# Input weights as two words: adding them on TensorE instead of GpSimd, in a three-layer attention and gating kernel

## The chip, the cores and the metric

The kernel runs on one core of one Trainium2 chip. The metric is the device time of one launch in microseconds, the median of the timed executions; it is to be small. The engines are named as in the profile: PE is TensorE's matmul, PEld its weight load, DVE is VectorE, ACT is ScalarE, POOL is GpSimd, SP is SyncE, which issues the DMAs here.

## The reference, cut to what matters

Three layers follow one another: an attention with two kinds of masks, a gated layer with a mixing over positions, and a mixture of four attention experts.

```python
q, k, v            # 4 batches, 8 heads, 576 positions, 64 columns, float32
a = softmax(where(mask_h, q @ k.T / 8, -1e9))     # heads 0-3: last 32 positions
x = concat_heads(a @ v)                           # heads 4-7: every 32nd position
h = maximum(x @ w_in, 0)                          # w_in: 512 x 1024, float64
u, v = h[..., :512], h[..., 512:]
v_n = (v - mean(v)) / sqrt(var(v) + 1e-6)
v_s = einsum('ts,bsd->btd', w_spatial, v_n) + b_spatial[None, :, None]
y = (u * v_s) @ w_out                             # w_out: 512 x 512, float64
# four experts: q, k, v = y @ wq[e], y @ wk[e], y @ wv[e]; causal attention;
# out = sum over the two experts with the largest gate of w_e * (a @ v @ wo[e])
```

In the first softmax the sum of a row gets 1e-9 added before it is inverted. The weights `w_in` and `w_out` come as float64, so a weight is read as two 32-bit words.

## The kernel before, in words

Every dense product is made of three matmuls on float32r operands: each operand is held as an upper part (`hi`, `wh`) and a remainder (`lo`, `wl`), and `mm3` (lines 274 to 283) adds hi by hi, lo by hi and hi by lo in one PSUM bank.

The order of all instructions is fixed when the program is built. A planner (class `Plan`, lines 33 to 148) takes steps from generators; a step yields the engine, or several to choose from with a cost each, the events it needs and the buffers it takes, and the planner gives each engine a list in the order in which the steps would start by these costs. So an engine runs its own list strictly in order and waits on semaphores for the others. The classes of buffers are `c` (75 tiles in SBUF), `w64` (raw weight words), `d`, `s`, `t`, `x` (the eight PSUM banks).

The first stage has two jobs side by side. For each of four head pairs of a batch the first attention runs: SP loads q, k and v, PE makes scores (line 467), DVE masks them and finds maxima (line 493), ACT takes the exponentials with row sums (line 499), DVE adds 1e-9 to the sums and inverts them (lines 502 and 503), POOL or DVE multiplies (line 506), PE transposes (line 524) and multiplies by v (line 565), and ACT and DVE split the result into `xh` and `xl` (lines 302 and 588). Meanwhile the eight tiles of `w_in`, 128 rows by 512 columns each, are prepared by `weight`. A tile of raw words is loaded into one of two `w64` buffers (line 329). DVE builds the value of its upper word as a float32 `a` in two instructions (336, 337), a power of two `p2` (338), and the remainder `m` from the lower word (341). Then the two are added on DVE or POOL (344), the sum is rounded to `hi` (302 on ACT, 304 on DVE or POOL), and `m` less `hi` gives `wl` on DVE or POOL (351). PE fills its idle time until a planned 46 us with matmuls on zeros (line 213).

The first dense products are `v_half` of batch 0 (lines 281 to 283, 512 columns), which need the second half of `w_in`, then `u_half` (288 columns), which needs all of the first half, and then the mixing over positions (`spatial`, lines 730 to 735). The attention of batch 1 is prepared by then, and from there on the batches follow each other. `w_out` and the experts' weights are prepared later, with the same function; `w_out` is float64 too.

Of the kernel before, what the change touches and what calls it, by code (L numbers as in the profile page):

```python
# [7 lines left out]
F = dt.float32  # L8
R = dt.float32r
I32 = dt.int32  # L10
AF = mybir.ActivationFunctionType
ALU = mybir.AluOpType
# [6 lines left out]
NCHUNK = 75  # L19
EXPERTS_AHEAD = 4  # L20
TAILS = 3
ALONE = 3
# [127 lines left out]
def fused(tc, qk, vl, vs, win, wsb, woutT, wp, wo, out):  # L150
# [5 lines left out]
        tc.tile_pool(name="ps", bufs=1, space=bass.MemoryType.PSUM),  # L156
    ]
    const, chunk, small, psum = [c.__enter__() for c in ctx]
    plan = Plan(dict(c=NCHUNK, w64=2, bd=TAILS, al=ALONE, ps=8, sq=PSUM_BANKS["d"] - 1, **PSUM_BANKS))
    plan.within = dict.fromkeys(PSUM_BANKS, "ps")  # L160

    n_names = [0]
# [1 line left out]
    def nm(s):  # L164
        n_names[0] += 1
        return f"{s}{n_names[0]}"

    def C(shape, dtype=F, name="c"):
        return chunk.tile(shape, dtype, name=nm(name), tag="c")

    def P(shape, tag):
        t = psum.tile([128, 512], F, name=nm("p" + tag), tag="p", bufs=8)
        n = 1
        for x in shape[1:]:
            n *= x
        t = t[: shape[0], :n]
        if len(shape) == 3:
            t = t.rearrange("p (a b) -> p a b", b=shape[2])
        return t
# [4 lines left out]
    def f(t):  # L184
        return t.bitcast(F)
# [7 lines left out]
    def t_dve(n, k=1, fixed=0.07):  # L193
        return k * fixed + n * 1.042e-3
# [4 lines left out]
    def t_pool(n, k=1):  # L199
        return k * 0.15 + n * 2.1e-3  # L200

    def t_mm(n, k):
        return k * max(n * 0.4167e-3 + 0.003, 0.056)
# [13 lines left out]

    ident = const.tile([128, 128], F, name="ident")
    make_identity(nc, ident)

    def keep(t, pattern, base, mult, cmp_op=ALU.is_ge, fill=NEG):
        pool.affine_select(t, t, pattern=pattern, base=base, channel_multiplier=mult, compare_op=cmp_op, fill=fill)
# [70 lines left out]
    def hi_of(n):  # L293
        return ("act", "dve", "pool"), (t_act(n), t_fast(n), t_pool(n))


    def out_of(n, k=1):
        return ("act", "dve"), (t_act(n, k), t_dve(n, k))

    def copy(out, in_):  # L300
        if plan.eng == "act":
            act.activation(out, in_, AF.Copy)  # L302
        else:
            engine().tensor_copy(out, in_)  # L304
# [7 lines left out]
    W = {}  # L312


    def weight(keys, src, r0, rows, c0, cols, after=()):


        n = len(keys)
        if src.dtype == F:
            yield "sp", 0.46, after, dict(c=1)  # L320
            m = C([rows, n * cols], F, "st")
            nc.sync.dma_start(m.rearrange("p (a c) -> p a c", a=n),
                              src[r0:r0 + n * rows, c0:c0 + cols].rearrange("(a p) c -> p a c", a=n))
            plan.dma(n * rows * cols * 4)
            plan.lat = 0.0
        else:
            yield "sp", 0.46, after, dict(w64=1)
            w = chunk.tile([rows, cols, 2], I32, name=nm("w64"), tag="w64", bufs=2)
            nc.sync.dma_start(w.rearrange("p a b -> p (a b)"),
                              src.bitcast(I32)[r0:r0 + rows, 2 * c0:2 * (c0 + cols)])  # L330
            plan.dma(rows * cols * 8)


            yield "dve", t_fast(2 * cols, 2) + t_dve(cols) + 0.25, (), dict(c=2)
            a, p2 = C([rows, cols], I32, "a"), C([rows, cols], I32, "p2")
            dve.tensor_scalar(a, w[:, :, 1], 3, 0x3FFFFFFF, op0=ALU.logical_shift_left, op1=ALU.bitwise_and)
            dve.scalar_tensor_tensor(a, w[:, :, 1], -0x40000000, a, op0=ALU.bitwise_and, op1=ALU.bitwise_or)
            dve.tensor_scalar(p2, a, -0x800000, None, op0=ALU.bitwise_and)
            yield "dve", t_dve(cols), (), dict(c=1)
            m = C([rows, cols], F, "m")  # L340
            engine().scalar_tensor_tensor(m, w[:, :, 0].bitcast(dt.uint32), 2.0 ** -52, f(p2), op0=ALU.mult, op1=ALU.mult)
            plan.give("w64")
            yield ("dve", "pool"), (t_dve(cols), t_pool(cols)), (), {}
            engine().tensor_add(m, m, f(a))
            plan.give("c", 2)
        yield *hi_of(n * cols), (), dict(c=1)
        hi = C([rows, n * cols], R, "wh")
        copy(hi, m)
        yield *lo_of(n * cols), (), dict(c=1)
        wl = C([rows, n * cols], R, "wl")  # L350
        engine().tensor_sub(wl, m, f(hi))
        plan.give("c")
        for i, key in enumerate(keys):
            W[key] = (hi[:, i * cols:i * cols + cols], wl[:, i * cols:i * cols + cols])
            plan.set(("W", key))
# [115 lines left out]
    def a1_weights(b, hp, g):  # L471
        local = hp < 2
        blocks = a1_blocks(hp, g)
        n = len(blocks)
        nk = 96 if local else 54
        width = [96 if local else min(54, S - 54 * j) for j in blocks]
        if not local:
            yield "pool", 0.25 + 0.25 * g, [("qk", b, hp)], dict(c=1)
            a = C([128, n + n % 2, 64], F, "a")
            pool.memset(a[:, :, 54:], 0.0)  # L480
            if g:
                pool.memset(a[:, 5, 36:], 0.0)
                pool.memset(a[:, 7, :54], 0.0)
        yield "dve", t_dve(n * nk, n), [("mask", local), ("s1", b, hp)], dict(c=1) if local else {}
        st = A1[b, hp]
        ps = st["ps"][g]

        mx = sm([128, 8], "mx")
        if local:
            a = C([128, n, nk], F, "a")  # L490
        for c, (j, w) in enumerate(zip(blocks, width)):
            m = mloc[:, min(j, 1)] if local else mstl if w == 36 else mstr
            dve.tensor_tensor_reduce(a[:, c, :w], ps[:, c, :w], m, op0=ALU.add, op1=ALU.min, scale=-0.125,  # L493
                                     scalar=3.0e38, accum_out=mx[:, c:c + 1])
        plan.give("s")
        yield "act", t_act(n * nk, n, 0.23), (), {}
        sums = sm([128, 8], "sums")
        for j, w in enumerate(width):
            act.activation(a[:, j, :w], a[:, j, :w], AF.Exp, bias=mx[:, j:j + 1], scale=-1.0,  # L499
                           accum_out=sums[:, j:j + 1])  # L500
        yield "dve", 0.3, (), {}
        dve.tensor_scalar_add(sums[:, :n], sums[:, :n], 1e-9)
        dve.reciprocal(sums[:, :n], sums[:, :n])
        yield ("dve", "pool"), (t_dve(n * nk), t_pool(n * nk)), (), {}
        x = a[:, :n, :nk]
        engine().tensor_mul(x, x, sums[:, :n].unsqueeze(2).broadcast_to([128, n, nk]))  # L506
        st["a"][g] = a
        plan.set(("a", b, hp, g))
# [656 lines left out]
    attention(0, 0)  # L1165
    for h in (1, 0):
        for k in range(4):
            plan.add(-0.5 + k if h else 2 + k, weight([("in", h, k)], win, 128 * k, 128, 512 * h, 512, after=() if h else ()))
    for s in range(4):
        plan.add(30, weight([("sp", s)], wsb, 128 * s, 128, 0, S, after=[("x",0,2,0)]))  # L1170
    plan.add(30, spatial_tail())
# [117 lines left out]
```

## Time and profile before

| | us |
|---|---|
| median of 3 timed runs | 456.47 (456.34 to 456.61) |
| the profiled execution's own time | 455.08 |
| span of the profiled execution | 453.2 |
| PE busy | 426.1 (94%) |
| DVE busy | 320.2 (71%) |
| ACT busy | 289.2 (64%) |
| POOL busy | 160.5 (35%) |

The span runs from the first instruction of the program to the last; the execution's own time holds what lies around it as well. The busy times are unions of instruction times on each engine. A busy PE is not a PE at its peak, since matmuls overlap and their ends are modelled, and the matmuls on zeros count as busy too.

### The profile page before, as it was taken

The page shows a single profiled execution, that of the slowest core. Times are in us where ns is not written, and L with a number is a line of the kernel's source. Part 1 is how long each engine was busy: PE and PEld are TensorE (multiplying, and loading weights), DVE is VectorE, ACT ScalarE, POOL GpSimd, SP SyncE. Part 2 cuts the span into 40 slices and gives each one's busy share as a digit, 9 for nine tenths or more (in the row PEclk, how much of TensorE's full clock was granted, in tenths as well). Part 3 has the DMA queues.
Part 4 walks back from the last instruction along what each step waited for, and adds up shares of the span by engine and source line. Part 5 has one row for each costly group of instructions (what it writes and reads, how often), then busy time and mean ns, then how long its engine had stood idle before and what let it go on. Part 6 is the DMA issues. An engine that isn't in the chain of part 4 may idle for free.

```text
span 453.2 us, 10964 instructions
## 1 busy us (share of the span) xinstructions
PE 426.1 (94%) x3872; PEld 382.7 (84%) x3872; DVE 320.2 (71%) x1145; ACT 289.2 (64%) x922; POOL 160.5 (35%) x248
## 2 busy tenths in 40 slices
PE   5786599999999999999999999999999999999796
PEld 2464478998899889999999999989998999988684
DVE  5999988246922485233999755679879898988861
ACT  3786789228950498331644433986878788878873
POOL 7766986022720163013669910102001222103200
PEclk9998989999999999999999999999999999999999
DMA  8988307300165000220200033810550370051234
GB/s 265 360 258 258 79 26 235 101 2 2 42 209 203 2 1 4 60 105 25 59 35 1 0 83 71 191 42 16 128 116 3 80 175 3 0 144 56 94 116 140
DMA packets 22554, 42.96 MB, mean 95 GB/s; under 512 B 3170, under 2 KB 5474, under 8 KB 22500
## 3 DMA queue, kind: packets, MB, share of 16 engines
q1 hardware_dynamic: 22500, 42.26, 32.8%
q8 instruction: 31, 0.51, 0.5%
q14 instruction: 23, 0.19, 0.1%
HBM read 26.00 MB, written 4.72 MB: 68 GB/s over the span
## 4 chain that ended last, share of the span: by engine, by line
PE 79%; DVE 11%; ACT 3%; POOL 3%; issue 2%; DMA 1%; POOLq 0%; ACTq 0%; DVEq 0%
PE pd L281 15%; PE pd L283 15%; PE pd L282 15%; PE pd L730 4%; PE pd L732 4%; PE pd L731 4%; PE pt L1010 4%; PE px L1055 2%; PE ps L925 2%; PE ps L926 2%; PE px L565 2%; PE pt L524 2%; PE px L1085 2%; PE px L1053 2%; PE ps L467 2%
## 5 line engine op out<-in xcount | busy, mean ns | idle before, releaser
L499 ACT ACTIVATE a<-a,mx 128x54 f32<-128x54 f32 (+2 forms) x160 | 54.4, 345 | 23.1 <-DVE mx L493 22.8
L946 POOL TENSOR_SCALAR a<-a,asums 128x128 f32<-128x128 f32 (+2 forms) x18 | 14.3, 802 | 96.5 <-ACT a L937 27.5
L738 DVE TENSOR_TENSOR u<-pd,u 128x288 f32<-128x288 f32 x32 | 14.2, 453 | 36.4 <-PE pd L735 36.2
L937 ACT ACTIVATE a<-a,amx 128x128 f32<-128x128 f32 (+1 forms) x64 | 35.5, 556 | 6.5 <-DVE amx L913 6.2
L281 PE MATMUL pd<-xh,wh 128*128 128x288 f32 x128 | 38.7, 302 | 0.1
L281 PE MATMUL pd<-gh,fh 128*128 128x288 f32 x128 | 38.0, 297 | 0.7 <-DVE cl L1070 0.7
L913 DVE CUSTOM_DVE_ANT_0 a<-ps,mqk 128x128 f32<-128x128 f32 (+4 forms) x72 | 33.0, 482 | 7.2 <-PE ps L926 5.7
L506 POOL TENSOR_TENSOR a<-a,sums 128x384 f32<-128x384 f32 (+3 forms) x30 | 24.7, 824 | 37.3 <-ACT a L499 14.1
L283 PE MATMUL pd<-gh,fl 128*128 128x288 f32 x128 | 37.9, 296 | 0.0
L730 PE MATMUL pd<-wh,vh 128*128 128x288 f32 x128 | 37.8, 295 | 0.0
L283 PE MATMUL pd<-xh,wl 128*128 128x288 f32 x128 | 37.7, 295 | 0.0
L282 PE MATMUL pd<-xl,wh 128*128 128x288 f32 x128 | 37.7, 294 | 0.0
L732 PE MATMUL pd<-wh,vlo 128*128 128x288 f32 x128 | 37.7, 294 | 0.0
L282 PE MATMUL pd<-gl,fh 128*128 128x288 f32 x128 | 37.7, 294 | 0.0
L731 PE MATMUL pd<-wl,vh 128*128 128x288 f32 x128 | 37.7, 294 | 0.0
L499 ACT ACTIVATION_READ_ACCUMULATOR a<-a,mx 128x1 f32 x160 | 30.5, 190 | 0.0
L999 DVE TENSOR_TENSOR e<-pt,e 128x384 fp32r<-128x384 f32 (+1 forms) x48 | 27.4, 597 | 4.0 <-ACT e L302 3.6
L281 PE MATMUL pd<-wh,xh 128*128 128x512 f32 x64 | 27.7, 432 | 0.4 <-DVE aT L304 0.4
L944 ACT ACTIVATE a<-a,asums 128x512 f32<-128x512 f32 (+3 forms) x46 | 26.5, 595 | 2.3 <-DVE asums L954 2.0
L653 POOL TENSOR_TENSOR rstd<-rstd,neghalf 128x1 f32<-128x1 f32 x18 | 11.5, 636 | 40.7 <-DVE rstd L651 25.7
L282 PE MATMUL pd<-wl,xh 128*128 128x512 f32 x64 | 25.7, 401 | 0.0
L283 PE MATMUL pd<-wh,xl 128*128 128x512 f32 x64 | 25.6, 399 | 0.0
(208 smaller groups left out, 1464.1 us busy)
## 6 DMA issues: line engine op xcount, KB each, us to landing
qk<-qk SPq DMA_DIRECT2D x64, 144.0 KB, 2.6
q<-in_qk_dram SPq DMA_DIRECT2D x16, 288.0 KB, 5.4
k<-in_qk_dram SPq DMA_DIRECT2D x16, 288.0 KB, 5.7
w<-in_win_dram SPq DMA_DIRECT2D x8, 512.0 KB, 5.7
out_dram<-o SPq DMA_DIRECT2D x16, 256.0 KB, 2.0
v<-in_vl_dram SPq DMA_DIRECT2D x16, 192.0 KB, 4.7
v<-in_vs_dram SPq DMA_DIRECT2D x8, 256.0 KB, 5.8
w<-in_woutT_dram SPq DMA_DIRECT2D x4, 512.0 KB, 6.4
```

The source lines that it names most:

```text
L281: pe.matmul(ps, ah, bh, start=i == 0, stop=False)
L282: pe.matmul(ps, ah, bl, start=False, stop=False)
L283: pe.matmul(ps, al, bh, start=False, stop=i == n - 1)
L499: act.activation(a[:, j, :w], a[:, j, :w], AF.Exp, bias=mx[:, j:j + 1], scale=-1.0, accum_out=sums[:, j:j + 1])
L506: engine().tensor_mul(x, x, sums[:, :n].unsqueeze(2).broadcast_to([128, n, nk]))
L730: pe.matmul(ps, vh[:, fs], wh[:, c0:c0 + cn], start=(i == 0), stop=False)
L731: pe.matmul(ps, vh[:, fs], wl[:, c0:c0 + cn], start=False, stop=False)
L732: pe.matmul(ps, vlo[:, fs], wh[:, c0:c0 + cn], start=False, stop=False)
L913: dve.tensor_tensor_reduce(a[:, s0:s0 + sn], ps, mask, op0=ALU.add, op1=ALU.min, scale=-0.125, scalar=m if s0 else 3.0e38, accum_out=m)
L937: act.activation(a, a, AF.Exp, bias=m, scale=-1.0, accum_out=st["sums", e][:, i:i + 1])
L944: act.activation(a, a, AF.Copy, scale=r)
L999: dve.tensor_sub(el, ps, f(eh))
```

## The change

For the eight tiles of `w_in` alone (`summed=True`) the sum is no longer made on POOL or DVE. `hi` is the rounded `a`, not the rounded sum. PE adds `a` times the identity, `m` times an identity in float32r and `hi` times a negative identity in one PSUM bank, and what stands there is copied out by ACT or DVE as `wl`. The first of these three matmuls takes float32 operands. `m` is now written as float32r. Two constants, `unit` and `minus`, are made by DVE at the start. The raw words have three buffers instead of two, for `w_in` and `w_out`. And the addition of 1e-9 to the row sums is written as an instruction that has the sums as both of its tensor inputs, (sums + 1e-9) max sums.

```diff
-    plan = Plan(dict(c=NCHUNK, w64=2, bd=TAILS, al=ALONE, ps=8, sq=PSUM_BANKS["d"] - 1, **PSUM_BANKS))
+    plan = Plan(dict(c=NCHUNK, w64=3, bd=TAILS, al=ALONE, ps=8, sq=PSUM_BANKS["d"] - 1, **PSUM_BANKS))
...
     make_identity(nc, ident)
+    unit, minus = (const.tile([128, 128], R, name=n) for n in ("unit", "minus"))
+    dve.tensor_copy(unit, ident)
+    dve.tensor_scalar_mul(minus, ident, -1.0)
...
-            w = chunk.tile([rows, cols, 2], I32, name=nm("w64"), tag="w64", bufs=2)
+            w = chunk.tile([rows, cols, 2], I32, name=nm("w64"), tag="w64", bufs=3)
...
-            m = C([rows, cols], F, "m")
+            m = C([rows, cols], R if summed else F, "m")
             engine().scalar_tensor_tensor(m, w[:, :, 0].bitcast(dt.uint32), 2.0 ** -52, f(p2), op0=ALU.mult, op1=ALU.mult)
             plan.give("w64")
+            if summed:
+                yield *hi_of(cols), (), dict(c=1)
+                hi = C([rows, cols], R, "wh")
+                copy(hi, f(a))
+                yield "pe", t_mm(cols, 6), (), dict(d=1)
+                ps = P([rows, cols], "d")
+                pe.matmul(ps, ident, f(a), start=True, stop=False)
+                pe.matmul(ps, unit, m, start=False, stop=False)
+                pe.matmul(ps, minus, hi, start=False, stop=True)
+                plan.give("c", 3)
+                yield *out_of(cols), (), dict(c=1)
+                wl = C([rows, cols], R, "wl")
+                copy(wl, ps)
+                plan.give("d")
+                key, = keys
+                W[key] = (hi, wl)
+                plan.set(("W", key))
+                return
             yield ("dve", "pool"), (t_dve(cols), t_pool(cols)), (), {}
             engine().tensor_add(m, m, f(a))
...
-        dve.tensor_scalar_add(sums[:, :n], sums[:, :n], 1e-9)
+        dve.scalar_tensor_tensor(sums[:, :n], sums[:, :n], 1e-9, sums[:, :n], op0=ALU.add, op1=ALU.max)
...
-            plan.add(-0.5 + k if h else 2 + k, weight([("in", h, k)], win, 128 * k, 128, 512 * h, 512, after=() if h else ()))
+            plan.add(-0.5 + k if h else 2 + k, weight([("in", h, k)], win, 128 * k, 128, 512 * h, 512, summed=True))
```

The planner makes the engines' lists anew. On POOL, at the end of the constants of the first stage (`mstl` is the last mask), before:

```order
L222 AFFINE_SELECT mstl<-mstl 64x36
L344 TENSOR_TENSOR m_174<-m_174,a_160 128x512
L351 TENSOR_TENSOR wl_246<-m_174,wh_230 128x512
L506 TENSOR_TENSOR a_213<-a_213,sums_233 128x480
L344 TENSOR_TENSOR m_284<-m_284,a_239 128x512
L506 TENSOR_TENSOR a_225<-a_225,sums_250 128x384
L351 TENSOR_TENSOR wl_352<-m_284,wh_314 128x512
```

and now (line numbers are the changed kernel's; 527 is the multiplication by the inverted sums, 501 to 504 are memsets):

```order
L225 AFFINE_SELECT mstl<-mstl 64x36
L527 TENSOR_TENSOR a_218<-a_218,sums_238 128x480
L527 TENSOR_TENSOR a_233<-a_233,sums_261 128x384
L501 MEMSET a_355 128x4x10
L501 MEMSET a_359 128x8x10
L503 MEMSET a_359 128x28
L504 MEMSET a_359 128x54
```

The additions of line 344 and the subtractions of line 351 are gone for all eight tiles of `w_in`; the multiplications that stood between them follow each other. Three of the eight roundings to `wh` come to POOL instead, later in its list.

On DVE, at the second tile of raw words, after the first nine maxima; before:

```order
L336 TENSOR_SCALAR a_239<-w_154 128x512
L337 SCALAR_TENSOR_TENSOR a_239<-w_154,a_239 128x512
L338 TENSOR_SCALAR p_240<-a_239 128x512
L502 TENSOR_SCALAR sums_233<-sums_233 128x5
L503 RECIPROCAL sums_233<-sums_233 128x5
L341 SCALAR_TENSOR_TENSOR m_284<-w_154,p_240 128x512
L502 TENSOR_SCALAR sums_250<-sums_250 128x4
L503 RECIPROCAL sums_250<-sums_250 128x4
```

and now:

```order
L339 TENSOR_SCALAR a_247<-w_158 128x512
L340 SCALAR_TENSOR_TENSOR a_247<-w_158,a_247 128x512
L341 TENSOR_SCALAR p_248<-a_247 128x512
L523 SCALAR_TENSOR_TENSOR sums_238<-sums_238 128x5
L524 RECIPROCAL sums_238<-sums_238 128x5
L344 SCALAR_TENSOR_TENSOR m_266<-w_158,p_248 128x512
L339 TENSOR_SCALAR a_269<-w_160 128x512
L340 SCALAR_TENSOR_TENSOR a_269<-w_160,a_269 128x512
L341 TENSOR_SCALAR p_270<-a_269 128x512
L523 SCALAR_TENSOR_TENSOR sums_261<-sums_261 128x4
L524 RECIPROCAL sums_261<-sums_261 128x4
L344 SCALAR_TENSOR_TENSOR m_307<-w_160,p_270 128x512
```

The third tile's four instructions (`w_160`, `a_269`, `p_270`, `m_307`) have moved up by nine maxima, to right behind the second's, and `sums` is added in the other form. The order of the engines' later work changes in the same manner; over the list up to the first maxima of batch 1's third head pair the work on DVE is the same but for one copy `wl<-pd`, one copy `xh<-px` of 256 columns and one multiplication of 384 columns more, and one copy `aT<-pt` of 256 columns less.

On PE, between the scores of the second and of the third head pair; before:

```order
L213 MATMUL pd_69<-zeros 128x512
L524 MATMUL pt_300<-ident,a_213 96x128 x4
L213 LDWEIGHTS zeros
L213 MATMUL pd_69<-zeros 128x512
L213 LDWEIGHTS zeros
L213 MATMUL pd_69<-zeros 128x512
L524 MATMUL pt_318<-ident,a_213 96x128
L467 MATMUL ps_320<-k_172,q_171 64x54
```

and now:

```order
L488 MATMUL ps_285<-k_163,q_162 64x96 x2
L545 MATMUL pt_309<-ident,a_218 96x128 x4
L352 MATMUL pd_315<-a_247,ident 128x512
L353 MATMUL pd_315<-m_266,unit 128x512
L354 MATMUL pd_315<-wh_276,minus 128x512
L545 MATMUL pt_348<-ident,a_218 96x128
L545 MATMUL pt_350<-ident,a_233 96x128 x4
L352 MATMUL pd_363<-a_269,ident 128x512
L353 MATMUL pd_363<-m_307,unit 128x512
L354 MATMUL pd_363<-wh_330,minus 128x512
L488 MATMUL ps_379<-k_210,q_209 64x54
```

The three matmuls of the second and of the third tile stand ahead of the third pair's scores, where matmuls on zeros were. Up to the first matmul of `spatial` PE's list has eight such groups of three more and 15 matmuls on zeros less (21 instead of 36), and is otherwise made of the same instructions.

## Rows read from the trace of the kernel before

**Rows 1.** Busy time by stretch: busy us (instructions), then PEclk, DMA share, GB/s.
```profile
2.00:45.00 43.00, 31.42 (x477) 20.37 (x476) 37.74 (x156) 27.75 (x130) 29.60 (x50) 0.97 0.94 297
4.70:57.30 52.60, 36.47 (x567) 25.14 (x567) 49.90 (x211) 36.26 (x158) 38.55 (x51) 0.95 0.80 248
85.80:292.00 206.20, 206.20 (x1928) 192.97 (x1927) 122.56 (x418) 104.94 (x348) 75.82 (x103) 1.00 0.21 59
```

**Rows 2.** Chain that ended last, 20 to 62 us, shares by line.
```profile
by line: DVE a L493 17.2%; DVE p L338 12.0%; DVE xl L588 10.0%; DVE a L337 9.5%; DVE a L336 9.2%; DVE sums L502 7.4%; issue 7.1%; DVE wl L351 5.9%; DVE m L341 5.9%; DVE a L506 4.3%; DVE xt L304 3.5%; DVE sums L503 3.4%; DVE bst L647 1.7%; D
```

**Rows 3.** Groups by shape, 4.7 to 57.3 us: busy us, mean ns, idle before.
```profile
L351 POOL TENSOR_TENSOR wl<-m,wh 128x512 fp32r<-128x512 f32 x8 | 11.5, 1438 | 2.0 <-ACT wh L302 1.8
...
L344 POOL TENSOR_TENSOR m<-m,a 128x512 f32<-128x512 f32 x8 | 10.6, 1329 | 5.5 <-DVE sums L502 3.5 <-DVE m L341 1.9
L213 PE MATMUL pd<-zeros 128*128 128x512 bf16 x27 | 8.1, 389 | 0.0
L336 DVE TENSOR_SCALAR a<-w 128x512 int32<-128x512 int32 x8 | 7.5, 935 | 3.9 <-DMA w<-in_win_dram 3.9
...
L341 DVE SCALAR_TENSOR_TENSOR m<-w,p 128x512 f32<-128x512 uint32 x8 | 6.4, 805 | 0.0
L338 DVE TENSOR_SCALAR p<-a 128x512 int32<-128x512 int32 x8 | 6.3, 788 | 0.3
...
L302 ACT ACTIVATE wh<-m 128x512 fp32r<-128x512 f32 x8 | 5.0, 626 | 9.3 <-POOL m L344 9.3
...
L502 DVE TENSOR_SCALAR sums<-sums 128x4 f32<-128x4 f32 x6 | 2.8, 469 | 0.0
...
L502 DVE TENSOR_SCALAR sums<-sums 128x7 f32<-128x7 f32 x2 | 1.3, 667 | 0.0
```

**Rows 4.** What reads tile a, to 60 us: ns min/median/max, first and last start.
```profile
L336 DVE TENSOR_SCALAR a<-w x8: 376/1040/1518, 4.7 to 48.2; 128x512 int32<-128x512 int32 x8
```

**Rows 5.** The same of tile p.
```profile
L338 DVE TENSOR_SCALAR p<-a x8: 426/427/1403, 5.9 to 50.3; 128x512 int32<-128x512 int32 x8
L341 DVE SCALAR_TENSOR_TENSOR m<-w,p x8: 652/676/1732, 6.4 to 51.0; 128x512 f32<-128x512 uint32 x8
```

**Rows 6.** Line 502 to 60 us, the same columns, forms.
```profile
L502 DVE TENSOR_SCALAR sums<-sums x13: 156/170/1174, 12.1 to 59.9; 128x4 f32<-128x4 f32 x7, 128x5 f32<-128x5 f32 x4, 128x7 f32<-128x7 f32 x2
```

**Rows 7.** Timeline of DVE: start us, duration us.
```profile
21.60 0.49 DVE L588 TENSOR_TENSOR xl<-px,xh 128x320 fp32r<-128x320 f32 x1
...
30.01 1.19 DVE L337 SCALAR_TENSOR_TENSOR a<-w,a 128x512 int32<-128x512 int32 x1
...
37.92 0.69 DVE L337 SCALAR_TENSOR_TENSOR a<-w,a 128x512 int32<-128x512 int32 x1
```

**Rows 8.** Timeline of POOL.
```profile
21.64 1.27 POOL L344 TENSOR_TENSOR m<-m,a 128x512 f32<-128x512 f32 x1
...
29.83 0.82 POOL L506 TENSOR_TENSOR a<-a,sums 128x378 f32<-128x378 f32 x1 [0.96 <-DVE sums L503]
...
37.66 0.28 POOL L482 MEMSET a<- 128x28 f32 x1
```

**Rows 9.** Line 304 on POOL, whole run: ns min/median/max.
```profile
L304 POOL CAST vh<-vr x3: 608/611/612, 69.8 to 168.3; 128x512 fp32r<-128x512 f32 x3
```

**Rows 10.** Line 304 on DVE, whole run.
```profile
L304 DVE COPY o<-pd x1: 685/685/685, 431.1 to 431.1; 128x512 f32<-128x512 f32 x1
```

**Rows 11.** Timeline of PE.
```profile
20.53 0.64 PE L524 MATMUL pt<-ident,a 128*96 128x128 f32 x4 [0.58 <-POOL a L506]
...
24.45 1.27 PE L565 MATMUL px<-aT,v 96*64 96x64 f32 x36
...
25.98 0.40 PE L282 MATMUL pd<-wl,xh 128*128 128x512 f32 x1
26.21 0.40 PE L283 MATMUL pd<-wh,xl 128*128 128x512 f32 x1
...
85.81 0.29 PE L730 MATMUL pd<-wh,vh 128*128 128x288 f32 x1
```

More of the change, by code (lines that the diff above doesn't have):

```diff
@@ L312, in fused, with weight @@
     W = {}
-    def weight(keys, src, r0, rows, c0, cols, after=()):
+    def weight(keys, src, r0, rows, c0, cols, after=(), summed=False):
         n = len(keys)
```

## The prediction

> **What bounds the kernel now.** I read busy time by stretch first, then the chain of waits, then the groups of the stretch that matters, and single rows last.
>
> From 85.8 to 292 us PE is busy for 206.20 of 206.20 us at a granted clock of 1.00 [rows 1]. Nothing that DVE, ACT or POOL save there can be seen in the time; and since the batches then follow each other on a full PE, the first matmul of the mixing over positions, at 85.81 us [rows 11], is a mark: what comes earlier there comes earlier at the end. The start is another matter. Between 4.7 us, when DVE first reads a raw tile [rows 4], and 57.3 us, DVE is busy for 49.90 of 52.60 us, PE for 36.47, ACT for 36.26 and POOL for 38.55 [rows 1]. The chain that ended last at 62 us names DVE's lines and almost nothing else [rows 2]. So DVE sets the end of this stretch. The transfers come close: their share is 0.94 from 2 to 45 us and 0.80 over the whole stretch [rows 1].
>
> DVE's busy time is not all work. The instruction of line 336 takes 376 ns at best and 935 on the mean of eight, that of 338 426 and 788, that of 341 652 and 805 [rows 3 to 5], and the addition to the sums takes 156 ns at best, but 469 on the mean of six and 667 on the mean of two [rows 3, 6]. The excess is 8 x 0.559 = 4.5, 8 x 0.362 = 2.9, 8 x 0.153 = 1.2, 6 x 0.313 = 1.9 and 2 x 0.511 = 1.0, in all 11.5 us. Single rows say what it is: line 337, which reads two SBUF tiles, took 1.19 us at 30.01 while POOL's multiplication ran from 29.83 to 30.65, and 0.69 at 37.92 beside a POOL memset, which only writes [rows 7, 8]. At 21.60 an instruction that reads PSUM took 0.49 for 320 columns, no longer than its size asks, in the middle of a POOL addition of 1.27 us [rows 7, 8]. So some DVE instructions wait until POOL has finished an instruction, others don't.
>
> **The change, part by part.**
>
> *POOL.* It loses eight instructions of line 344 at 1.329 and eight of 351 at 1.438 us [rows 3], 22.1 us. It gains three roundings to `wh`; the nearest row is the cast of the same size, 0.611 us [rows 9], so 1.8 us. Its busy time in the stretch goes from 38.55 to about 18.3. If DVE's waits go in proportion to what POOL executes, 11.5 x 18.3 / 38.55 = 5.5 us of them stay and 6.0 go. The bounds: at least a quarter goes, 2.9, since for less today's multiplications, masks and memsets, 16.4 of POOL's 38.55 us, would have to cause over three quarters of the waits; at most all go, 11.5. I take 6.0.
>
> *DVE.* By the order it has in the stretch one copy `wl<-pd` more, 0.69 us by the copy of 512 columns from PSUM [rows 10]; a copy `xh<-px` of 256 columns more and a copy `aT<-pt` of 256 less, which cancel; and a multiplication of 384 columns more, 0.6 by the 0.49 for 320 columns [rows 7]. Sum +1.3 us; between 0.7 (the multiplication moved from a time when DVE is idle) and 1.8 (it waits for POOL). The two new constants are made before 4.7 us, where DVE stands idle for most of the 3.9 us that it waits for raw words [rows 3]: nothing; without that idle time they would be two copies of 128 columns, about 0.35 us by a quarter of [rows 10] each.
>
> *The sums' new form.* At 4 or 7 columns an instruction is all overhead, so I take 156 to 170 ns [rows 6] for it as well. What could change is the wait. Its two inputs are now both in SBUF, as those of line 337, which waited for POOL's multiplication and not for its memset [rows 7, 8]. So I let it wait for multiplications as before, and give the saving no term of its own: below nothing it can't go by more than a few tens of ns each, and above lie the whole 2.9 us of the old form's waits, of which half is in the 6.0 already.
>
> [...]
>
> *PE.* Eight groups of three matmuls of 512 columns are new. The two in float32r cost 0.23 us each, the distance of 25.98 and 26.21 [rows 11]. For the float32 one I have two rows: four transpositions of 128 columns, 512 in all, in 0.64 us, and 36 records of 64 columns in 1.27 us [rows 11], which is 0.28 for 512 columns or 0.56 if a matmul makes two passes. I take 0.6, between 0.23 (no slower than float32r) and 1.3 (two passes of the dearer row). A group is 1.06 us, eight are 8.5 us, between 5.5 and 14. They are covered: PE's idle time in the stretch is 52.60 - 36.47 = 16.1 us [rows 1], and of its busy time 8.1 us in 27 instructions are matmuls on zeros [rows 3], of which 15 go (4.5 us). Without cover the price would be the 8.5 us. Cost 0.
>
> *ACT.* By the order it copies seven of the eight `wl` out of PSUM, 0.63 us each by its roundings of the same size [rows 3], and gives three roundings away: +4 x 0.63 = 2.5 us, against idle time of 16.3 us [rows 1]. And its roundings no longer wait for POOL's sum, the cause of 9.3 us of that idle time [rows 3]; `wl` of a tile is ready when `m` is there and three matmuls and a copy have run (about 1.7 us) instead of after 1.33 + 0.63 + 1.44 = 3.4 us on three engines, each with its queue. This takes no time from DVE, but keeps the first dense product from becoming the late one.
>
> *The third raw buffer.* A tile of raw words can be loaded one tile earlier. Its 128 x 512 x 8 bytes are 0.52 MB, 1.8 us at the 297 GB/s of [rows 1]; they stand ahead of a head pair's q and k, whose scores then come up to 1.8 us later. What is late next is a maximum on DVE; DVE then works on the raw tile, which is there. I take 0, bounds -0.5 (line 336's 3.9 us of idle time [rows 3] is in part the second tile's) and +1.8.
>
> **The sum.** -6.0 + 1.3 = -4.7 us before 57.3 us, passed on whole by a full PE: the mark moves from 85.8 to about 81.1, the span from 453.2 to 448.5. The profiled execution took 455.08 us, so 450.4 for its like; the median shown is 1.39 above the profiled execution, so 451.8 for the median.
>
> **The rivals.**
>
> *A larger gain.* DVE's waits nearly vanish, because the sums' new form does not wait or because what POOL has left falls beside maxima, which read PSUM. For: at 21.60 a reader of PSUM passed [rows 7, 8], and by the order DVE's maxima are many. Against: line 337's wait was for a multiplication, and all of these stay. Then -9.5 + 1.3 = -8.2: 448.3 us. Chance 0.15.
>
> *The gain is lost.* DVE gets its time back, but another bound stands right behind it: the transfers at a share of 0.94 [rows 1]. With a tile of raw words every so often and q, k, v of the pairs in between, an earlier DVE waits for words, as it does for 3.9 us on line 336 now [rows 3]. For: the share. Against: it falls after 45 us, to give the 0.80 of the whole stretch, so the last tiles are there in time, and DVE's end is later than the words'. The gain is then between 0 and 2 us: 455.5 us. Chance 0.15.
>
> *PE turns into the bound, and it gets slower.* PE works through its list strictly in order. The three matmuls of the second and third tile stand ahead of the third pair's scores, and wait for `m` from DVE and `hi` from ACT; behind them wait the scores, behind those DVE's maxima. And with 15 fewer matmuls on zeros PE is idle more often. [...] For: PE's list. Against: each group of three takes matmuls with it that keep PE as busy as the zeros did, 8.5 against 4.5 us. Chance 0.10.
>
> *The change doesn't do what it says*: waits go, but DVE isn't what sets the end. The chain of [rows 2] speaks against it; its time is that of the lost gain, and it is counted there.
>
> **How the numbers follow.** The forecast, a gain of 2 to 7.5 us, has 0.60; alone it spans 449.0 to 454.5. The larger gain has 0.15, the lost gain 0.15, the slower case 0.10. About 0.2%, 0.9 us, is what a measurement of this kernel can tell from no change. All of the forecast and of the larger gain is faster, and a third of the lost gain: 0.80. The rest of the lost gain is the same: 0.10; slower 0.10. For 8 in 10 the range takes the forecast, most of the larger gain (down to 447.3) and that part of the lost gain up to 456.0.
>
> **What would show it.** In the changed kernel's profile: POOL busy some 18 us up to 57 us; the instruction of the old line 336 on a mean near 0.6 us, not 0.94; eight `wl` from PSUM without a long wait on DVE or ACT; a float32 matmul by the identity near 0.6 us; the sums' addition over 0.3 us only beside a POOL multiplication; the granted clock above 0.9 in the stretch; the first matmul of the mixing near 81 us, and PE busy without a gap from there. I am wrong if DVE stands idle for raw words or for scores by more than 5 us up to 57 us, if POOL's multiplications follow so closely that the wait per DVE instruction stays the same, or if PE waits for `m` or `hi` while scores stand behind.

## The result, and the profile after

| | us |
|---|---|
| before, median of 4 | 456.54 (456.34 to 458.01) |
| changed, median of 4 | 450.26 (447.89 to 455.52) |
| changed, once more, median of 6 | 450.04 (447.81 to 453.32) |
| before beside it, median of 23 | 456.54 (455.18 to 459.15) |

The ratio is 0.9833 (0.98 to 0.9866) the first time and 0.9869 (0.9827 to 0.9912) the second: 7.6 and 6.0 us faster, where 4.7 were forecast; the medians lie 6.3 and 6.5 us apart. The ratios leave out executions more than 1.5% longer than the fastest of their kernel: that of 455.52 us here, and below those of 607.6 us (granted clock 0.659) and 464.61 us of `pe_sum_only` and that of 463.17 us of `pool_reads`. The first profiled execution of the changed kernel took 455.52 us, with a granted clock of 0.50 from 48 to 54 us and 0.86 from 54 to 56, and again of 0.82 from 420 to 425 and 0.50 from 425 to 430, so the rows below are from the profiled execution of the repeat, 450.11 us. Its first line, and busy time by stretch, in the columns of [rows 1]; the last stretch begins with the first matmul of the mixing:

```profile
span 448.3 us, 10983 instructions
```
```profile
2.00:45.00 43.00, 38.38 (x494) 24.64 (x496) 36.61 (x175) 32.54 (x141) 18.28 (x43) 1.00 1.04 314
4.70:57.30 52.60, 46.05 (x645) 31.88 (x649) 47.19 (x227) 42.28 (x179) 26.70 (x55) 0.97 0.82 247
80.50:287.00 206.50, 206.50 (x1929) 193.33 (x1929) 122.92 (x419) 106.54 (x351) 76.17 (x104) 1.00 0.21 60
```

DVE is busy for 47.19 us instead of 49.90, POOL for 26.70 instead of 38.55, and PE for 46.05 instead of 36.47. From 57.3 to 287 us PE has no idle time at all; before, it had some until 75 us. The groups by shape up to 57.3 us, in the columns of [rows 3]; lines 339, 341, 344 and 523 were 336, 338, 341 and 502:

```profile
L352 PE MATMUL pd<-a,ident 128*128 128x512 f32 x16 | 9.0, 648 | 0.1
...
L344 DVE SCALAR_TENSOR_TENSOR m<-w,p 128x512 fp32r<-128x512 uint32 x8 | 5.4, 680 | 0.0
...
L305 ACT ACTIVATE wl<-pd 128x512 fp32r<-128x512 f32 x7 | 4.2, 594 | 0.0
...
L339 DVE TENSOR_SCALAR a<-w 128x512 int32<-128x512 int32 x8 | 4.1, 516 | 3.3 <-DMA w<-in_win_dram 3.3
...
L341 DVE TENSOR_SCALAR p<-a 128x512 int32<-128x512 int32 x8 | 3.4, 427 | 0.3
L213 PE MATMUL pd<-zeros 128*128 128x512 bf16 x10 | 3.3, 456 | 0.1
...
L523 DVE SCALAR_TENSOR_TENSOR sums<-sums 128x4 f32<-128x4 f32 x7 | 3.1, 439 | 0.5 <-ACT a L520 0.5
...
L523 DVE SCALAR_TENSOR_TENSOR sums<-sums 128x7 f32<-128x7 f32 x2 | 0.3, 160 | 0.0
```

The mean of line 339 is 516 ns (935 before), that of 341 is 427 (788), that of 344 is 680 (805). What is left of DVE's excess is 8 x 0.14 on line 339, and on the sums' additions 7 x 0.28: with the few hundredths of line 344 some 3.3 us of 11.5. On the sums of four columns nothing is gained, 439 ns against 469; the two of seven are at 160 and had waited before.

The chain that ended last at 62 us, to be held against [rows 2], and the timeline of PE, with a group of the new matmuls, PE's longest wait, and the mark:

```profile
by line: DMA q<-in_qk_dram 15.3%; DVE a L514 12.6%; DVE a L340 6.6%; PE pd L286 6.6%; PE pd L284 6.5%; DVE xl L609 6.0%; PE ps L488 5.9%; PE px L586 5.7%; DVE sums L523 5.6%; PE pt L545 5.6%; PE pd L285 5.4%; issue 4.3%; DVE m L344 4.2%; DV
```
```profile
41.90 1.02 PE L352 MATMUL pd<-a,ident 128*128 128x512 f32 x2
42.35 0.80 PE L353 MATMUL pd<-m,unit 128*128 128x512 f32 x1
42.99 0.39 PE L354 MATMUL pd<-wh,minus 128*128 128x512 f32 x1
43.22 0.60 PE L545 MATMUL pt<-ident,a 128*96 128x128 f32 x4
...
47.05 0.50 PE L286 MATMUL pd<-wh,xl 128*128 128x512 f32 x1 [1.93 <-DVE xl L609]
...
80.47 0.29 PE L751 MATMUL pd<-wh,vh 128*128 128x288 f32 x1
```

The chain is no longer DVE's alone: a transfer of `q` and PE's dense products (lines 284 to 286) stand in it. The group that begins at 41.90 ends, for the next instruction, at 43.22: 1.32 us. Its float32 matmul is two records in the trace (16 for the eight tiles), as the 18 float32 matmuls of line 565 for a pair of nine blocks and two heads are 36 records in [rows 11]. The mark is at 80.47 us, 5.3 before that of [rows 11].

### The profile page after: what moved, and what is told of

It is laid out like the page before. It is cut to its first block, busy times and chain, and to the rows that moved or that the text cites. A ratio compares the mean times of both kernels' runs of the same rounds, so it can differ in the third digit from the quotient of the medians.

```text
span 453.8 us, 10987 instructions
## 1 busy us (share of the span) xinstructions
PE 438.0 (97%) x3889; PEld 390.9 (86%) x3889; DVE 312.6 (69%) x1147; ACT 291.8 (64%) x926; POOL 140.7 (31%) x236
## 4 chain that ended last, share of the span: by engine, by line
PE 85%; DVE 8%; DMA 3%; ACT 1%; issue 1%; SPq 0%; DVEq 0%; ACTq 0%
PE pd L284 16%; PE pd L286 16%; PE pd L285 16%; PE pt L1031 4%; PE pd L751 4%; PE pd L753 4%; PE pd L752 4%; PE ps L488 3%; PE px L586 3%; PE pt L545 2%; DMA w<-in_win_dram 2%; PE px L1076 2%; PE px L1106 2%; PE ps L946 2%; PE ps L947 2%; PE px L1074 2%
## 5 line engine op out<-in xcount | busy, mean ns | idle before, releaser
L520 ACT ACTIVATE a<-a,mx 128x54 f32<-128x54 f32 (+2 forms) x160 | 54.5, 349 | 22.3 <-DVE mx L514 22.1
L527 POOL TENSOR_TENSOR a<-a,sums 128x216 f32<-128x216 f32 (+3 forms) x30 | 24.9, 830 | 49.3 <-ACT a L520 15.8
L751 PE MATMUL pd<-wh,vh 128*128 128x288 f32 x128 | 37.7, 295 | 0.0
L286 PE MATMUL pd<-xh,wl 128*128 128x288 f32 x128 | 37.7, 295 | 0.0
L285 PE MATMUL pd<-xl,wh 128*128 128x288 f32 x128 | 37.7, 295 | 0.0
L753 PE MATMUL pd<-wh,vlo 128*128 128x288 f32 x128 | 37.7, 294 | 0.0
L752 PE MATMUL pd<-wl,vh 128*128 128x288 f32 x128 | 37.7, 294 | 0.0
L285 PE MATMUL pd<-gl,fh 128*128 128x288 f32 x128 | 37.7, 294 | 0.0
L609 DVE TENSOR_TENSOR xl<-px,xh 128x108 fp32r<-128x108 f32 (+4 forms) x48 | 19.3, 433 | 12.6 <-ACT xh L305 12.5
L305 ACT ACTIVATE e<-pt 128x384 fp32r<-128x384 f32 (+1 forms) x48 | 23.8, 522 | 3.1 <-PE pt L1031 2.5
```

The costliest lines, as they stand in the source:

```text
L285: pe.matmul(ps, ah, bl, start=False, stop=False)
L286: pe.matmul(ps, al, bh, start=False, stop=i == n - 1)
L751: pe.matmul(ps, vh[:, fs], wh[:, c0:c0 + cn], start=(i == 0), stop=False)
L752: pe.matmul(ps, vh[:, fs], wl[:, c0:c0 + cn], start=False, stop=False)
L753: pe.matmul(ps, vlo[:, fs], wh[:, c0:c0 + cn], start=False, stop=False)
```

## The experiments

The ratio is to executions of the kernel before, timed beside each kernel. Among the executions of one kernel the longer ones mostly have the lower mean granted clock (of the 23 of the kernel before beside the repeat, the five of 458.3 us and more have 0.978 or 0.981, the six of 455.8 and less 0.983 to 0.991), so medians that differ by a microsecond say little, and where it matters executions of like clock are compared.

**What each edit does.** In `new_sums_only` the kernel before gets the new form of the sums' addition, in `old_sums` the changed kernel gets the old one. Neither moves an instruction.

```diff
-        dve.tensor_scalar_add(sums[:, :n], sums[:, :n], 1e-9)
+        dve.scalar_tensor_tensor(sums[:, :n], sums[:, :n], 1e-9, sums[:, :n], op0=ALU.add, op1=ALU.max)
```

> The kernel before with the new form of the sums' addition and nothing else, the order unchanged. Theory (two SBUF inputs wait for POOL's instructions that read, which here are nearly all): within 1 us of before. Rival (the form is what counts): 2 to 3 us faster.

> The changed kernel with the sums' addition in its old form, the order of all instructions unchanged. Theory (the new form still waits for POOL's multiplications): within 1 us of the changed kernel. Rival (the new form is what waits less): 2 to 3 us slower than the changed kernel, and the addition's mean well over the changed kernel's 0.44 us.

Measured: 457.06 us, ratio 0.9995 (0.9973 to 1.0016), and 449.19 us, 0.9856 (0.9816 to 0.9896). The form is worth nothing that can be measured on either side. In the changed kernel's own trace the new form waits as line 337 did: beside POOL's subtractions it took 1.36 us, about until the first of them ended, and beside a memset 0.15. DVE first, then POOL:

```profile
42.91 1.36 DVE L523 SCALAR_TENSOR_TENSOR sums<-sums 128x4 f32<-128x4 f32 x1
...
49.33 0.15 DVE L523 SCALAR_TENSOR_TENSOR sums<-sums 128x5 f32<-128x5 f32 x1
```
```profile
42.83 2.80 POOL L372 TENSOR_TENSOR wl<-st,wh 128x576 fp32r<-128x576 f32 x2
...
49.10 0.32 POOL L266 MEMSET bd<- 128x256 f32 x1
```

**The third raw buffer** alone on the kernel before, and the changed kernel without it (and with the old sums):

```diff
-    plan = Plan(dict(c=NCHUNK, w64=2, ...
+    plan = Plan(dict(c=NCHUNK, w64=3, ...
...
-            w = chunk.tile([rows, cols, 2], I32, name=nm("w64"), tag="w64", bufs=2)
+            w = chunk.tile([rows, cols, 2], I32, name=nm("w64"), tag="w64", bufs=3)
```

> The kernel before with three raw buffers and nothing else. Theory: DVE is bound by work and waits for POOL, so an earlier raw tile gives nothing: 455.5 to 458 us. Rival (third buffer): 2 to 4 us faster than before, 452.5 to 454.5 us.

> Only the sum on TensorE: two raw buffers and the old form of the sums' addition. Theory (the work that POOL lost is the gain): still 4 to 7 us faster than before, 450 to 453 us. Rival (the third raw buffer is what DVE needed, since the transfers bound it next): 1 to 3 us faster than before at most, 454 to 456 us.

Measured: 458.64 us, 1.0054 (1.0029 to 1.008), and 460.23 us, 1.0065 (1.0039 to 1.0092). Each alone makes the kernel slower; both together, `old_sums`, are 11 us faster than the sum on TensorE alone. Both expectations fell. PE's rows of `pe_sum_only` show why:

```profile
53.49 0.68 PE L545 MATMUL pt<-ident,a 128*118 128x128 f32 x2 [3.47 <-POOL a L527]
53.97 1.92 PE L352 MATMUL pd<-a,ident 128*128 128x512 f32 x2
54.90 1.42 PE L353 MATMUL pd<-m,unit 128*128 128x512 f32 x1
56.11 0.63 PE L354 MATMUL pd<-wh,minus 128*128 128x512 f32 x1
...
58.79 2.08 PE L352 MATMUL pd<-a,ident 128*128 128x512 f32 x2
```
```profile
30.00:45.00 15.00, 12.38 (x119) 9.14 (x119) 13.01 (x55) 13.16 (x56) 8.74 (x16) 0.77 0.99 309
45.00:60.00 15.00, 10.96 (x137) 7.53 (x137) 11.04 (x49) 11.04 (x47) 9.49 (x20) 0.74 0.02 7
```

The order that the planner makes for two buffers puts five of the eight groups behind 53 us (here those at 53.97 and 58.79; the others begin at 63.5, 66.6 and 68.0), where PE has no idle time left to hide them: from 53.5 us to the mark it is busy without a gap. In the changed kernel all eight are done at 43.2 us; DVE begins the last tile at 37.7 us there, not at 48.8. And PE's wait of 3.47 us for POOL's multiplication is followed by matmuls at half pace: the float32 pair takes 1.92 us, where 1.02 is its time in the changed kernel. The granted clock is 0.50 from 54 to 60 us; its mean is 0.77 from 30 to 45 us and 0.74 from 45 to 60. The mark comes at 90.6 us. No run shows why the third buffer costs 2 us when it stands alone.

**How much of that is the clock?** The same kernel with matmuls on zeros in PE's two longest waits:

```diff
             if eng == "pe" and st < self.WARM:
                 self.fill(st - self.t["pe"])
+                self.n_pe = getattr(self, "n_pe", 0) + 1
+                if self.n_pe == 28:
+                    self.fill(6.5 * 0.4268)
             elif eng == "pe" and self.warming:
+                self.fill(15.5 * 0.4268)
                 self.warming = False
```

> The sum on TensorE alone (two raw buffers, old form of the sums' addition), with matmuls on zeros in its two longest waits of PE: six ahead of the third pair's scores at 34 us and fifteen ahead of the transpositions that wait for POOL until 53.5 us. In the run without them some 17 us before the mark had a granted clock of 0.50. Theory (two raw buffers are slow through the clock, which PE's waits let fall): 4 to 8 us faster than without them, 452 to 456 us. Rival (the order itself, with four of the eight tiles' sums behind 53 us, is what costs): within 2 us of 460.

Measured: 459.44 us, 1.0049 (1.0028 to 1.0071). In its profile the granted clock is 1.00 from 30 to 75 us and the mark at 87.1 us. That is 3.5 earlier than without zeros, but the execution that was profiled there was one of the longer ones (463.76 us); the medians differ by 0.8 us. So in the main it is the order that costs, not the clock. `old_sums` differs from `pe_sum_only` in the number of buffers alone, and in its profile, too, the clock is 1.00 from 30 to 75 us; its mark is at 79.9 us. The mark with zeros is 7.2 us later, and five groups of 1.32 us are 6.6.

**POOL's work by itself.** The kernel before with lines 344 and 351 left out for `w_in` (`hi` is then the rounded lower part alone, and stands in for `wl`), everything else in its order, two buffers, nothing new on PE:

```diff
-            engine().tensor_add(m, m, f(a))
+            if src is not win:
+                engine().tensor_add(m, m, f(a))
...
-        wl = C([rows, n * cols], R, "wl")
-        engine().tensor_sub(wl, m, f(hi))
+        if src is win:
+            wl = hi
+        else:
+            wl = C([rows, n * cols], R, "wl")
+            engine().tensor_sub(wl, m, f(hi))
```

> The kernel before with the additions of line 344 and the subtractions of line 351 left out for w_in (hi is the rounded lower part alone, and stands in for wl too), the order of everything else unchanged, two raw buffers, nothing new on TensorE. POOL loses 22 us. [...] Rival (the order that three raw buffers bring is the gain): within 2 us of before.

Measured: 449.59 us, 0.9846 (0.982 to 0.9871), mark at 79.1 us. The whole gain is there without any of the change's other parts, and not through the clock: at a like clock it is 5 to 7 us. The 22 us that POOL no longer works are what the start paid for. The changed kernel, with its new matmuls and its own order, is as fast, 450.0 against 449.6. The edit also makes `hi` and `wl` ready sooner; that this alone is not the gain is shown by the next two kernels, which keep the changed kernel's way to `hi` and `wl` and lose all of it. PE's waits for POOL's multiplications are about halved, not gone. Up to the mark they were, in the kernel before, in this one, in the changed kernel, and in the first of the next two (us, times, longest):

```profile
PE pt L524 <- POOL a L506: 4.4, 6, 1.4
PE pt L528 <- POOL a L510: 2.3, 4, 0.7
PE pt L545 <- POOL a L527: 1.1, 2, 0.6
PE pt L547 <- POOL a L529: 5.4, 4, 2.1
```

Then the work given back to POOL in the changed kernel, once as additions that read SBUF, once as memsets that only write:

```diff
             plan.give("w64")
             if summed:
+                for _ in range(2):
+                    pool.tensor_add(f(p2), f(a), f(a))
```
```diff
             plan.give("w64")
             if summed:
+                for _ in range(5):
+                    pool.memset(f(p2), 0.0)
```

> The changed kernel, and for each tile of w_in POOL makes two additions of 512 columns once m is there, whose result nobody reads: about the work that the change took from it, and nothing else comes back. Theory (DVE's waits for POOL are the gain): most of it is lost, 454 to 457 us, and the mean of the instructions on lines 339 and 341 is back near 0.8 us. Rival (the gain comes from the order, or from a sum that is ready sooner): within 1.5 us of the changed kernel.

> The changed kernel, and for each tile of w_in POOL makes five memsets of 512 columns once m is there: as long as the two additions, but reading nothing. [...] Rival (it is POOL being busy that counts, since its multiplications come later): as slow as with the additions.

Measured: 458.5 us, 1.002 (0.9995 to 1.0044), mark 89.1, and 460.48 us, 1.0077 (1.0052 to 1.0103), mark 91.0. Both take back all of the gain, with the additions more than the theory had for them; for the memsets the rival came true. With the additions DVE waits again, though less on lines 339 and 341 (0.55 and 0.65 us) than expected and most on line 340, which has two SBUF inputs:

```profile
L348 POOL TENSOR_TENSOR p<-a 128x512 f32<-128x512 f32 x16 | 17.5, 1096 | 11.3 <-DVE m L344 9.4 <-DVE sums L525 1.2
...
L340 DVE SCALAR_TENSOR_TENSOR a<-w,a 128x512 int32<-128x512 int32 x8 | 8.9, 1114 | 0.3
```

With the memsets DVE hardly waits. The groups of that kernel, up to 60 us, its chain from 20 to 62 us, and what PE waited for up to its mark:

```profile
L348 POOL MEMSET p<- 128x512 f32 x40 | 22.3, 557 | 9.7 <-DVE m L344 7.8
...
L340 DVE SCALAR_TENSOR_TENSOR a<-w,a 128x512 int32<-128x512 int32 x8 | 6.2, 776 | 0.3
...
L341 DVE TENSOR_SCALAR p<-a 128x512 int32<-128x512 int32 x8 | 4.2, 523 | 0.4
L339 DVE TENSOR_SCALAR a<-w 128x512 int32<-128x512 int32 x8 | 3.9, 487 | 2.8 <-DMA w<-in_win_dram 2.8
...
L525 DVE SCALAR_TENSOR_TENSOR sums<-sums 128x4 f32<-128x4 f32 x5 | 2.0, 398 | 0.0
```
```profile
by line: POOL p L348 16.1%; PE pd L354 9.6%; DVE a L516 6.8%; DVE xl L611 6.6%; PE pt L547 6.5%; POOL a L529 6.5%; PE ps L490 6.0%; PE px L588 5.2%; DVE sums L525 5.1%; DVE m L344 4.8%; issue 4.5%; PE pd L286 3.3%; PE pd L284 2.6%; DVE wl L
```
```profile
PE pt L547 <- POOL a L529: 8.1, 4, 2.5
...
PE pd L356 <- POOL wh L307: 1.4, 1, 1.4
```

Line 340, with two SBUF inputs, is at 776 ns beside the memsets as in the changed kernel, line 339 at 487; DVE's excess (8 x 0.11, 8 x 0.10, 5 x 0.24) is 2.9 us, no more than the changed kernel's 3.3. With the additions the excess is some 8.5 us, of which 2.7 are line 340's. The memsets, at 22.3 us, are 4.8 us more work for POOL than the additions, at 17.5, and the kernel is 2 us slower. What the memsets do is to stand in POOL's queue, and first in the chain with 16.1%, ahead of the multiplications, for which PE's transpositions wait 8.1 us and PE's third matmul of a group 1.4; and they hold the queue for another 9.7 us in which they wait for `m` themselves, where the additions of line 344 in the kernel before waited 5.5 [rows 3]. So a loss of this size needs no added wait of DVE's: the queue alone can make it.

**DVE's work by itself.** The kernel before without line 338 (the power of two is left out, `a` itself is the factor), in the same order:

```diff
-            dve.tensor_scalar(p2, a, -0x800000, None, op0=ALU.bitwise_and)
...
-            engine().scalar_tensor_tensor(m, w[:, :, 0].bitcast(dt.uint32), 2.0 ** -52, f(p2), op0=ALU.mult, op1=ALU.mult)
+            engine().scalar_tensor_tensor(m, w[:, :, 0].bitcast(dt.uint32), 2.0 ** -52, f(a), op0=ALU.mult, op1=ALU.mult)
```

> The kernel before with line 338 left out (the power of two; line 341 multiplies by a instead), the order unchanged: DVE loses eight instructions of 0.43 us, 3.4 us, and 2.9 us of waits in them. Theory of the prediction (DVE sets the end of the first stretch): 3 to 6 us faster. Rival (POOL's late multiplications and PE's order set it): less than 1.5 us faster.

Measured: 456.85 us, 0.9982 (0.9955 to 1.0009), in two clusters: four of twelve executions at 452.3 to 453.4 us with a granted clock of 0.987 to 0.992, eight at 456 to 457.8 with 0.977 to 0.985. Executions of the kernel before at 0.987 to 0.991 took 455.1 to 456.7 us (six of nineteen). So with the higher clock 5 us less on DVE up to the mark (64.59 us busy against 69.61) are worth about 3 us. In the other eight executions next to nothing is left: the seven at 0.977 and 0.978 have a mean of 457.3 us, the one of the kernel before at 0.977 took 457.9. On the median the rival came true, in the upper cluster the theory.

**PE's cover, and the clock of the changed kernel.** The float32 matmul made twice, and nine matmuls on zeros in PE's wait at 45.8 us:

```diff
-                pe.matmul(ps, ident, f(a), start=True, stop=False)
+                pe.matmul(ps, ident, f(a), start=True, stop=True)
+                pe.matmul(ps, ident, f(a), start=True, stop=False)
```
```diff
+LAST = 36
...
+                self.n_pe = getattr(self, "n_pe", 0) + 1
...
             pe.matmul(ps, ah, bl, start=False, stop=False)
+            if plan.warming and plan.n_pe == LAST and n == 4:
+                fill(9.5 * 0.4268)
```

> The changed kernel with the float32 matmul by the identity made twice for each tile of w_in, 8 x 1.16 = 9.3 us more of TensorE by the profile of the changed kernel (16 records in 9.3 us). Theory (the new matmuls are covered by idle time and zeros): less than 2 us slower. Rival (PE has become the second bound): 5 to 9 us slower.

> The changed kernel with nine matmuls on zeros put into the longest wait of PE, between the second and the third matmul of one product at 45.8 us (2.3 us in one execution, 1.9 in another, each followed by 4 to 7 us of granted clock 0.50). Theory (what varies between executions is the clock after that wait): no stretch at 0.50 near 48 to 52 us, 1 to 3 us faster than the changed kernel, 447 to 449 us, and less spread. Rival (clock falls for another reason, or DVE sets the end there): within 0.7 us of the changed kernel, or slower by the 2 us of zeros.

Measured: `more_pe` 452.49 us, 0.9899 (0.9866 to 0.9932), 2.4 us slower than the changed kernel by the medians and 1.4 by the ratios, nearer to the theory than to the rival. The eight matmuls added are 6.9 us, not 9.3: the second of two float32 matmuls starts 0.86 us after the first (rows in the last section), and the durations of the records overlap. So two thirds or more of them are covered, not all. `zeros_in_wait` 449.55 us, 0.9839 (0.9814 to 0.9864), no faster than the changed kernel's 450.04 by what can be told; the 447 to 449 us expected were missed. The stretches after the wait, first in the changed kernel and then with the zeros (and a late stretch of the latter):

```profile
46.00:48.00 2.00, 0.95 (x26) 0.67 (x28) 2.00 (x12) 1.81 (x12) 1.80 (x5) 0.97 0.10 35
48.00:50.00 2.00, 2.00 (x34) 1.80 (x29) 1.97 (x19) 1.46 (x9) 1.44 (x5) 0.50 0.00 0
50.00:52.00 2.00, 2.00 (x9) 1.55 (x9) 1.93 (x16) 0.40 (x1) 1.87 (x4) 0.68 0.00 0
```
```profile
46.00:48.00 2.00, 1.74 (x41) 0.94 (x40) 2.00 (x12) 1.50 (x9) 1.80 (x5) 1.00 0.04 12
48.00:50.00 2.00, 2.00 (x29) 1.70 (x22) 1.97 (x21) 1.41 (x9) 1.44 (x5) 1.00 0.00 0
50.00:52.00 2.00, 2.00 (x36) 1.50 (x36) 1.93 (x14) 2.00 (x10) 1.87 (x4) 1.00 0.00 0
420.00:430.00 10.00, 10.00 (x45) 8.56 (x45) 5.34 (x18) 6.07 (x13) 1.61 (x2) 0.67 0.35 112
```

The half clock after the wait is gone, as expected, and the mark is at 78.8 us, 1.7 earlier; this execution then lost it again between 420 and 430 us, after PE had stood idle for 2.8 us in all between 410 and 420. The two executions with a mean granted clock of 0.999 took 448.5 us.

> The changed kernel once more, for its spread and for a profile with less of the lower TensorE clock in it. The first four times lay between 447.9 and 455.5 us, the mean granted clock between 0.985 and 0.995. Theory (DVE waits less for POOL): 448 to 451 us, the first mixing matmul near 81 us, and whatever lies between two executions is time at the lower clock. Rival (the gain comes from somewhere behind 86 us): the mark stays near 83 us and the rest of the gain lies behind it.

Measured as in the first table: the mark is at 80.5, and the rest of the gain does not lie behind it: from the mark to the end of the span there are 367.8 us, 367.4 before. Between executions the time goes with the clock: 447.8 to 450.1 us at 0.995, 452.65 at 0.985, 453.3 at 0.981.

## Why the prediction was right, and where not

**The sum.** Forecast was a mark at 81.1 and a time of 451.8 us; measured were 80.5 and 450.0 to 450.3. That the size comes so near is in part luck. POOL's missing work took 8.2 us of DVE's waits away, not 6.0, and DVE's busy time up to the mark fell by 8.8; handed on one to one, as the prediction had it, that would have moved the mark by more than the 5.3 us that it moved. And of the 6.5 us between the medians some 2 go with a higher granted clock, which the sum did not hold. That is an estimate from two executions of the repeat, 453.32 us at 0.981 and 452.65 at 0.985: they lie 5.1 and 3.9 us below the kernel before's means at 0.981 and 0.984 (458.4 and 456.6). The other four had 0.995, the kernel before at most 0.991. What the prediction took from line 337 for the new form of the sums came true: it waited for a reading POOL instruction (1.36 us at 42.91) and not for a memset (0.14 us in `pool_writes` at 27.04, in a row of memsets). Line 337, now 340, took 0.69 us there at 13.90, 29.36, 34.68 and 45.50, each time within such a row; the memset of [rows 8] that the prediction took for this ended 0.02 us after line 337 had begun, and showed little.

**The step that held only in part: "So DVE sets the end of this stretch".** The prediction turned DVE's saved waits one to one into time. `before_less_dve` shows that a microsecond off DVE is worth about 0.6 in its four executions with the higher clock, and nothing that can be told on the median. `pool_writes` shows that 22 us on POOL can cost as much without DVE's waits, by standing ahead of the multiplications that PE's transpositions need. `no_pool_sums` shows that POOL's work is the cause of the gain; how much of it goes by DVE's waits and how much by POOL's queue to PE stays open. By 0.6, DVE's 8.8 us less busy time up to the mark (60.85 against 69.61) would be some 5 of the 6.5 us, on the median of `before_less_dve` next to none; and the memsets of `pool_writes`, in rows of 3 us, may weigh more in the queue than the instructions that the change removed: they add 7.0 us to PE's waits for the multiplications of the changed kernel, while the change had taken 3.3 us from them. The chain of [rows 2] showed DVE's lines because DVE is the last link in nearly every step of it; it did not show that POOL is in the same loop.

**"The third raw buffer. I take 0".** Wrong in kind. Alone it costs 2 us, and without it the rest of the change costs 3.7 us instead of giving 6.5. It was judged as a buffer, by when a transfer could start, and not as a number from which the planner makes the order: it decides whether the eight groups lie before 44 us (`old_sums`) or five of them behind 53 us (`pe_sum_only`).

**"Covered ... Cost 0" for PE.** Right for this order, as far as 450.0 against 449.6 in another order without the matmuls can show it, at a group of 1.32 us, not 1.06, so 10.6 us and not 8.5: the term mis-sized is the float32 matmul, 0.86 us by `more_pe` and not 0.6. The price named for the case that the cover is gone, 8.5 us for eight groups, is of the size of the 7.2 us by which the mark of `pe_sum_zeros` lies behind that of `old_sums`, with five groups uncovered.

**The rivals.** The lost gain through the transfers did not come, though their share is 1.04 up to 45 us and a transfer stands in the chain. The slower case came with two buffers (460.2 us), and in the main not through the clock: with zeros, at a granted clock of 1.00 from 30 to 75 us, it is still 459.4, and it is the uncovered groups that cost. POOL's busy time was to be 18.3 us and is 26.7: work that stood behind 57 us has moved up. One sign of being wrong was just met if its two parts are added: DVE stood idle for 3.3 us for raw words and 2.1 for scores, 5.4 against the 5 named (3.9 and 1.0 before). The sums' addition took over 0.3 us beside a POOL subtraction too. The other signs came as forecast: line 339 near 0.6 us (0.516), clock above 0.9 (0.97), PE without a gap from the mark.

## What to carry to other kernels

A chain of waits names the engine that came last at each step, not the one whose work would shorten the loop: before a saving is booked, take work from each engine of the loop in turn, as `no_pool_sums` and `before_less_dve` do, since they answered 7.1 us and, on the median, nothing. Work that moves to an engine with idle time is free only while the order puts it into that idle time; here one buffer count decided over 11 us (449.2 us in `old_sums`, 460.2 in `pe_sum_only`). Where a planner makes the order from such counts, read the new order at the places of the cover, not only the engine's sum of idle time.

## What the runs showed of the hardware that was not expected

In `pool_writes` line 339, with one SBUF input, waited beside two rows of five POOL memsets for less than one of them, 0.42 and 0.13 us. DVE first and then POOL:

```profile
27.04 0.14 DVE L525 SCALAR_TENSOR_TENSOR sums<-sums 128x4 f32<-128x4 f32 x1
...
28.49 0.84 DVE L339 TENSOR_SCALAR a<-w 128x512 int32<-128x512 int32 x1
29.36 0.69 DVE L340 SCALAR_TENSOR_TENSOR a<-w,a 128x512 int32<-128x512 int32 x1
...
34.10 0.55 DVE L339 TENSOR_SCALAR a<-w 128x512 int32<-128x512 int32 x1
```
```profile
26.78 3.02 POOL L348 MEMSET p<- 128x512 f32 x5 [0.61 <-DVE m L344]
...
32.10 3.01 POOL L348 MEMSET p<- 128x512 f32 x5 [0.61 <-DVE m L344]
```

Line 339 takes 0.42 us when it is free (at 11.05, with no POOL instruction running), and 0.84 and 0.55 in the middle of rows of memsets that ran 3.0 us, in which one memset takes 0.56; the sums' addition in its new form took 0.14 beside them.

And the float32 matmul by the identity costs more than the start of the next record lets it seem. In the group shown at 41.90 the second matmul starts 0.45 us after the first, but the third only 0.64 us after the second, though both are float32r, of which one otherwise follows the other in 0.23 [rows 11]. In `more_pe`, where one float32 matmul stands behind another, the distance is 0.86 us:

```profile
19.64 1.02 PE L352 MATMUL pd<-a,ident 128*128 128x512 f32 x2
20.50 1.02 PE L353 MATMUL pd<-a,ident 128*128 128x512 f32 x2
```

With 0.23 for each of the two others that makes the 1.32 us of the group, so its float32 matmul can be counted at 0.86 us, and nothing shows that it slows the others.
